# A fused attention and expert kernel: three of eighteen score steps kept whole instead of six, with work moved between ScalarE, VectorE and GpSimd

## Chip, core and metric

The kernel runs on one core of a Trainium2 chip. The metric is device time in microseconds (us) of one launch. Three runs of the kernel before took 906.69 us (median; 906.01 to 906.83).

## The reference

There are two stages. The first is attention over 4 batches and 8 heads (32 in all), with 1152 keys, 64 numbers per head, and queries averaged in pairs, so that 576 are left:

```
q_pool = q.reshape(B, H, S // 2, 2, D).mean(axis=3)
scores = matmul(q_pool, k.T) / sqrt(D);  scores -= max(scores, axis=-1)
attn = exp(scores);  attn /= sum(attn, axis=-1) + 1e-9
x = matmul(attn, v)
```

The second takes the 2304 rows of x (512 wide) through `h = x @ w_in`, `g = s * max(h, 0)**2 + b`, `out = g @ w_out`, with 2048 columns in between. Everything is float32.

## The kernel before

**Splitting.** A float32r matmul stands as one record in the trace, a plain float32 one as two (384 records for the 192 of L774). To keep accuracy with float32r the kernel splits a tile into a rounded part (names that end in h: `ph`, `kh`, `qh`, `xh`; for values `vv`) and what the rounding left (`pl`, `vl`), and multiplies high by high, high by low and low by high. The rounded part is a copy into a float32r tile (`hi_of`); the rest is a subtraction.

**Steps.** The attention goes head by head, each head in 9 steps of 128 keys (`NJ`), so that two heads, a pair, are 18 steps, numbered 0 to 17 here, and there are 16 pairs. `score_step` multiplies keys by queries (four float32r matmuls, L742) into a PSUM tile `s`, of which there are two: the scores of a step need the tile of the step two before. ScalarE takes the exponential from it. The table `KIND` says by step what follows:

- `w`, whole: one exponential into `pe` (L746), kept in float32. `value_step` multiplies it with the unsplit values `vf` by two float32 matmuls (L774).
- `v`: a rounded exponential `ph` (L751) and a full one in place in PSUM (L754); VectorE subtracts to `pl` (L757) and by that frees the tile `s`. `value_step` has six float32r matmuls (L780, L782, L784).
- `g`: the same, but the full exponential goes to `pe` in SBUF, which frees `s` at once, and GpSimd subtracts. The matmuls are the same six.

`value_step` runs three steps behind (`LAG`). TensorE also runs the units that find the row maximum ahead of time (`max_unit`, L687, one or two in a step); VectorE reduces them (L688).

**Preparation.** While a pair runs, the operands of the pair after the next are made, at steps that the table `PREP` gives: transposes on VectorE (`ka`, `kb`, `qt`), rounding (`ha`, `hb`, `qh`), the low parts on GpSimd (`kl`, `ql`), `qz0` and `qz1` (`q_blocks`: a rounded copy of 64 partitions by 512 queries that gathers every fourth, for the maximum units), `qm` (a corner copy on ScalarE), and the transfers into place `l0`, `l1` from the queue of SyncE. `FIRST` shifts some in the first pair. `prep_v` rounds the values of the next head (`vv`) and subtracts (`vl`), at steps 8 and 17 (`VS`). `XT` and `STA` say how many steps after their start the pieces of the normalisation and of a weight's conversion come.

Each engine runs its instructions strictly in the order written; the tables set that order. `later(k, fn)` writes fn's instructions k steps on.

Of the kernel before, what the change touches and what calls it, by code (L numbers as in the profile page):

```python
# [32 lines left out]
KB = 384  # L33


KIND = "wvwvgvwvg" + "vwgvwvwgv"

PP = (("ka", 2), ("kb", 3), ("ha", 3), ("hb", 4), ("qs", 3), ("qt", 4), ("qm", 5), ("qz", 5), ("qh", 6), ("ql", 7), ("kl", 7), ("l0", 8))
FIRST = {"qs": 4, "qt": 1, "qm": 1, "qh": 1, "qz": 1, "ql": 1, "l1": 4}
PREP = (("qs", 9), ("ka", 10), ("kb", 11), ("ha", 11), ("hb", 12), ("kl", 12), ("qt", 13), ("qm", 14), ("qh", 14), ("qz", 14), ("ql", 15), ("l0", 4), ("l1", 13))  # L40
LR = 14
LD = 5
VS = (8, 17)
XT = (2, 2, 3, 4, 8)
SW = (3, 8)
CB, CP = 270, 18
WB = (7, 7)
STA = (0, 1, 3, 5, 8, 9, 18, 19, 20)
STB = (0, 1, 2, 3, 4, 5, 5, 7, 9)
MO = (2, 3, 6)  # L50
MP = (1, 2, 3, 4, 6)
# [5 lines left out]
def f32(ap):  # L57
    return ap.bitcast(F32)
# [3 lines left out]
def attention_moe_kernel(ctx: ExitStack, tc: tile.TileContext, q, k, v, w_in, w_out, s_in, b_in, out):  # L62
    nc = tc.nc
# [5 lines left out]
    P = 128  # L69
# [3 lines left out]
    NT4 = SQ // P  # L73
# [217 lines left out]
    def hi_of(eng, out, in_):  # L291
        if eng is nc.scalar:
            nc.scalar.activation(out, in_, AF.Copy)  # L293
        else:
            eng.tensor_scalar(out=out, in0=in_, scalar1=1.0, scalar2=0.0, op0=ALU.mult, op1=ALU.add)
# [6 lines left out]
    def later(k, fn):  # L302
        step[1] += 1
        queue.append((step[0] + k, step[1], fn))
# [217 lines left out]
    qm = ap.tile([P, P], F32R, name="qm")  # L522

    qzs = [ap.tile([P, 2, NT4 * P], F32R, name=f"qz{i}") for i in range(2)]
# [4 lines left out]
    def side(hd, of="v"):  # L529

        h = hd % 2 if of == "v" else 1 - hd % 2
        return slice(h * D, (h + 1) * D)
# [19 lines left out]
    def load_q(p, which=(0, 1)):  # L552
        if p not in qraw:
            qraw[p] = ap.tile([P, NBQ, 2, 32], F32, tag="qraw", name=f"qraw{p}")
        for r, b, h, c in quarters(p):
            for e in which:
                eng = nc.sync if p > 1 or e == 0 else nc.scalar
                eng.dma_start(qraw[p][r, :, e], q[b, h, e::2, c].rearrange("(j t) i -> t j i", t=32))
# [6 lines left out]
    def prep_pair(p):  # L565

        kr, qr = kraw.pop(p), qraw.pop(p)
        kT = ap.tile([P, S], F32, tag="kT", bufs=2, name=f"kT{p}")
        qT = ap.tile([P, SQ], F32, tag="qT", bufs=2, name=f"qT{p}")
        qs = ap.tile([P, NBQ, 32], F32, tag="qs", name=f"qs{p}")  # L570
        kh = ap.tile([P, S], F32R, tag="kh", bufs=2, name=f"kh{p}")
        qh = ap.tile([P, SQ], F32R, tag="qh", bufs=2, name=f"qh{p}")
        krv = kr.rearrange("p j i -> p (j i)")
        lo, hi = (slice(0, SQ), slice(SQ, S)) if p else (slice(0, KB), slice(KB, S))

        def corner():
            assert holds.get("qm", -1) == p - 1
            for h in range(2):
                d = slice(h * D, (h + 1) * D)
                hi_of(nc.scalar, qm[d, d], qT[d, NT4 * P:])  # L580
            holds["qm"] = p

        def k_hi(part, last):
            hi_of(nc.scalar if p < 3 else nc.gpsimd, kh[:, part], kT[:, part])
            khs[p] = kh

        def q_hi():
            hi_of(nc.scalar if p < 2 else nc.gpsimd, qh, qT)
            qhs[p] = qh

        def q_blocks(h):
            r = slice(h * D, (h + 1) * D)
            to, of = qzs[p % 2][r, h], (f32(qh) if p == 0 and h else qT)[r, :NT4 * P]
            if p or h:
                hi_of(nc.scalar if p == 0 else nc.gpsimd, to.rearrange("p (t m) -> p t m", t=NT4), of.rearrange("p (m t) -> p t m", t=NT4))
            else:
                hi_of(nc.gpsimd, to, of)

        def both():
            q_blocks(0)  # L600
            q_blocks(1)

        def k_lo(part=slice(0, S)):
            nc.gpsimd.tensor_tensor(out=kT[:, part], in0=kT[:, part], in1=f32(kh[:, part]), op=ALU.subtract)

        def lay(h):
            hd = 2 * p + h
            kk, qq = kks[hd % 3], qqs[hd % 3].rearrange("p i a n -> p i (a n)")
            r = slice(h * D, (h + 1) * D)
            def k_hi_to(part):  # L610
                nc.sync.dma_start(f32(kk[0:D, :, part]), f32(kh[r, part]).unsqueeze(1).to_broadcast([D, 2, part.stop - part.start]))

            def k_lo_to(part):
                nc.sync.dma_start(f32(kk[D:P, 0, part]), kT[r, part])

            def q_hi_to():
                nc.sync.dma_start(f32(qq[0:D, 0, :]), f32(qh[r]))
                nc.sync.dma_start(f32(qq[D:P, 0, :]), f32(qh[r]))

            if hd == 0:  # L620
                for part in (lo, hi):
                    nc.sync.dma_start(f32(kk[0:D, 0, part]), f32(kh[r, part]))
                nc.scalar.activation(kk[0:D, 1], f32(kh[r]), AF.Copy)
                q_hi_to()
                k_lo_to(lo)
                k_lo_to(hi)
                nc.sync.dma_start(f32(qq[0:D, 1, :]), qT[r])
            else:
                k_lo_to(slice(0, S))
                k_hi_to(slice(0, S))  # L630
                q_hi_to()
                nc.sync.dma_start(f32(qq[0:D, 1, :]), qT[r])
            holds["k", hd % 3] = hd

        return {
            "ka": lambda: nc.vector.transpose(out=kT[:, lo], in_=krv[:, lo]),
            "qs": lambda: (nc.vector if p < 2 else nc.gpsimd).tensor_tensor(out=qs, in0=qr[:, :, 0, :], in1=qr[:, :, 1, :], op=ALU.add),
            "kb": lambda: nc.vector.transpose(out=kT[:, hi], in_=krv[:, hi]),  # L638
            "ha": lambda: k_hi(lo, False),
            "qt": lambda: nc.vector.transpose(out=qT, in_=qs.rearrange("p j i -> p (j i)")),  # L640
            "hb": lambda: k_hi(hi, True),
            "qh": q_hi,
            "qz": both,
            "qz0": lambda: q_blocks(0),
            "qz1": lambda: q_blocks(1),
            "kla": lambda: k_lo(lo),
            "klb": lambda: k_lo(hi),
            "kl": k_lo,
            "ql": lambda: nc.gpsimd.tensor_tensor(out=qT, in0=qT, in1=f32(qh), op=ALU.subtract),
            "qm": corner,  # L650
            "l0": lambda: lay(0),
            "l1": lambda: lay(1),
        }

    def prep_v(hd):
        vf, vv, vl = vfs[hd % 2][:, :, side(hd)], vvs[hd % 2][:, :, side(hd)], vls[hd % 2]
        if hd % 2:
            vl = vl[:, :, side(hd)]
        hi_of(nc.gpsimd, vv, vf)

        def lo():
            nc.gpsimd.tensor_tensor(out=vl, in0=vf, in1=f32(vv), op=ALU.subtract)  # L662
            holds["v", hd % 2] = hd

        later(1, lo)
# [123 lines left out]
    def finish(hd, a):  # L789
# [34 lines left out]
        if h == 0:  # L824
            later(XT[0], invert)
        else:
            for at, fn in zip(XT, (invert, reciprocal, spread, scale, send)):
                later(at, fn)
# [38 lines left out]
    for n in range(AHEAD):  # L867
        for u in range(begun(n - AHEAD), begun(n - AHEAD + 1)):
            max_unit(u, *((ps_m, "m") if u % 2 == 0 else (ps_s, "s")))
            if u == 1:  # L870
                prep["qz1"]()
                load_q(1, (1,))
                load_k(1)
                load_q(1, (0,))
                prep["l1"]()
                zeros(1)
                constants(1)
                prep_v(0)
                ones(1)
                constants(2)  # L880
        tick()
        if n == 11:
            prep = prep_pair(1)

    moe = Moe()
    lays = {}
    weights_a = conversions(wa, wstage, 0, SW[0], 1, STA, parts=2)
    NS = NH * NJ

    for n in range(NS + LAG):  # L890
# [5 lines left out]
        for part in ORDS.get(n % 18, ORD[at]) if at is not None else "sff":  # L896
            if part == "s" and n < NS:
                score_step(hd, j, KIND[n % 18])
            elif part == "f":
# [10 lines left out]
        if n < NS:  # L910
            p, h = divmod(hd, 2)
# [3 lines left out]
            if n == LD:  # L915
# [3 lines left out]
                load_q(2)  # L919
            if n % 18 == PREP[0][1]:  # L920
                lays = {k: prep[k] for k in ("l0", "l1") if k in prep}
                prep = prep_pair(p + 2) if p + 2 < NPAIR else {}
            for name, at in PREP:

                ops = prep if name not in ("l0", "l1") or at < PREP[0][1] else lays
                if n % 18 == at + (0 if p else FIRST.get(name, 0)) and name in ops and n >= 8:
                    ops.pop(name)()
# [134 lines left out]
```

## Time and profile before

| | us |
|---|---|
| median of 3 runs | 906.69 |
| the profiled execution | 906.96 |
| span of its core, first to last instruction | 905.1 |
| TensorE busy | 886.2 |
| VectorE busy | 690.8 |
| GpSimd busy | 637.2 |
| ScalarE busy | 573.9 |

The profiled execution spent 1.9 us outside its span. PE is the matmul side of TensorE and PEld its weight loads, DVE is VectorE, ACT ScalarE, POOL GpSimd, SP SyncE. The attention runs from about 20 to 500 us, the experts from there to the end. The granted clock of TensorE has mean 0.999 over the span.

### The profile page before, as it was taken

The numbers are of one execution on the slowest core, as the hardware profiler recorded it, in microseconds if no ns is written. First come the engines' busy times: TensorE is split into PE (matmuls) and PEld (weight loads), VectorE is DVE, ScalarE is ACT, GpSimd is POOL, SyncE is SP. The second block draws the span as 40 slices with busy tenths as digits, with TensorE's granted clock in tenths as the row PEclk, the third lists the DMA queues.
The fourth block names the chain that finished last, engine by engine and source line by source line (L and its number), as shares of the span: only waits on it lengthen the run. The fifth ranks groups of instructions, "written<-read, shape, count | busy, mean of one in ns | idle before, by whom it ended". The sixth has DMA issues, their size and how long they took to land.

```text
span 905.1 us, 17064 instructions
## 1 busy us (share of the span) xinstructions
PE 886.2 (98%) x6036; PEld 832.5 (92%) x6036; DVE 690.8 (76%) x1272; ACT 573.9 (63%) x1055; POOL 637.2 (70%) x541
## 2 busy tenths in 40 slices
PE   5999999999999999999999999999999999999997
PEld 3899999999999999999998899989999999999997
DVE  5888888889888988898874788789884456666666
ACT  3767667777776767776778677766664445454443
POOL 7767867887888788878856667579985445555443
PEclk9999999999999999999999999999999999999999
DMA  8889788877978797879563466766534222222111
GB/s 158 155 173 190 163 163 172 166 173 158 188 150 178 158 192 144 180 159 181 130 146 97 154 195 209 216 197 212 187 135 133 78 70 72 71 71 70 48 47 47
DMA packets 255733, 130.93 MB, mean 145 GB/s; under 512 B 203744, under 2 KB 227424, under 8 KB 255648
## 3 DMA queue, kind: packets, MB, share of 16 engines
q1 hardware_dynamic: 248544, 128.96, 60.2%
q10 hardware_dynamic: 7104, 0.89, 0.7%
q8 instruction: 48, 0.79, 0.4%
q14 instruction: 37, 0.30, 0.1%
HBM read 68.68 MB, written 18.87 MB: 97 GB/s over the span
## 4 chain that ended last, share of the span: by engine, by line
PE 94%; DVE 2%; ACT 1%; DMA 1%; POOL 1%; issue 0%; ACTq 0%; POOLq 0%; DVEq 0%
PE s L742 17%; PE h L412 11%; PE y L387 11%; PE h L360 11%; PE o L774 10%; PE seven L460 10%; PE m L687 8%; PE o L782 5%; PE o L784 5%; PE o L780 5%; DVE pm L688 1%; DMA kraw<-in_k_dram 0%; DMA qraw<-in_q_dram 0%; DVE kT L638 0%; DVE lt L802 0%
## 5 line engine op out<-in xcount | busy, mean ns | idle before, releaser
L688 DVE TENSOR_REDUCE pm<-m 128x1 f32<-128x384 f32 x432 | 227.6, 545 | 55.2 <-PE m L687 49.5
L742 PE MATMUL s<-qq,kk 128*128 128x288 f32 x1152 | 215.5, 309 | 1.9 <-DVE qq L716 1.3
L742 PEld LDWEIGHTS s<-qq,kk 128*128 128x128 f32 x1152 | 176.1, 190 | 13.9 <-ACT qq L714 1.6
L751 ACT ACTIVATE ph<-s 128x576 fp32r<-128x576 f32 x192 | 125.3, 653 | 91.9 <-PE s L742 91.1
L687 PE MATMUL m<-kh,qz 128*128 128x384 f32 x384 | 152.3, 409 | 0.5 <-DVE pm L688 0.5
L757 POOL TENSOR_TENSOR pl<-pe,ph 128x576 fp32r<-128x576 f32 x64 | 91.2, 1425 | 79.6 <-ACT pe L754 54.1
L774 PE MATMUL o<-pe,vf 128*128 128x288 f32 x384 | 120.9, 405 | 0.0
L757 DVE TENSOR_TENSOR pl<-s,ph 128x576 fp32r<-128x576 f32 x128 | 95.9, 749 | 23.0 <-ACT s L754 17.8
L782 PE MATMUL o<-ph,vl 128*64 128x288 f32 (+1 forms) x384 | 113.3, 295 | 0.2 <-POOL vl L662 0.2
L784 PE MATMUL o<-pl,vv 128*128 128x288 f32 x384 | 113.2, 295 | 0.1
L780 PE MATMUL o<-ph,vv 128*128 128x288 f32 x384 | 113.0, 294 | 0.0
L360 PE MATMUL h<-x,wih 128*128 128x256 f32 x576 | 106.8, 283 | 0.8 <-DVE gl L374 0.7
L412 PE MATMUL h<-x,wih 128*128 128x256 f32 x576 | 104.2, 281 | 0.0
L360 PEld LDWEIGHTS h<-x,wih 128*128 128x128 f32 x576 | 93.7, 190 | 7.7 <-DVE gl L374 1.9
L440 POOL TENSOR_TENSOR cl<-c,ch 128x640 fp32r<-128x640 f32 x35 | 54.9, 1567 | 56.3 <-ACT ch L436 56.3
L412 PEld LDWEIGHTS h<-x,wih 128*128 128x128 f32 x576 | 88.7, 188 | 0.2
L754 ACT ACTIVATE s<-s 128x576 f32<-128x576 f32 x128 | 83.6, 653 | 0.0
L687 PEld LDWEIGHTS m<-kh,qz 128*128 128x128 f32 x384 | 73.4, 194 | 9.3 <-DVE pm L688 2.9
L338 POOL TENSOR_TENSOR x<-xr,x 128x1024 fp32r<-128x1024 f32 x27 | 64.9, 2405 | 23.8 <-ACT x L293 23.8
L360 PE MATMUL h<-x,wil 128*128 128x256 f32 x288 | 81.6, 283 | 0.0
L412 PE MATMUL h<-x,wil 128*128 128x256 f32 x288 | 81.1, 282 | 0.0
L746 ACT ACTIVATE pe<-s 128x576 f32<-128x576 f32 x96 | 62.7, 653 | 25.7 <-PE s L742 21.2
(295 smaller groups left out, 2196.1 us busy)
## 6 DMA issues: line engine op xcount, KB each, us to landing
kk<-kh SPq DMA_DIRECT2D x31, 576.0 KB, 6.4
vf<-in_v_dram SPq DMA_DIRECT2D x32, 288.0 KB, 4.5
qq<-qh SPq DMA_DIRECT2D x64, 144.0 KB, 5.6
xr<-xd SPq DMA_DIRECT2D x18, 512.0 KB, 3.9
kk<-kT SPq DMA_DIRECT2D x31, 288.0 KB, 3.4
qraw<-in_q_dram SPq DMA_DIRECT2D x120, 72.0 KB, 2.5
kraw<-in_k_dram SPq DMA_DIRECT2D x60, 144.0 KB, 3.4
wsti<-in_moe_w_in_dram SPq DMA_DIRECT2D x13, 512.0 KB, 4.0
```

The source lines that it names most:

```text
L360: nc.tensor.matmul(h[:, :TB], st[:, c, :], mv[:, c, :], start=(n == 0), stop=(n == 3 * NC - 1))
L387: nc.tensor.matmul(y[:, :DM], st[:, ts_], mv, start=(first and n == 0), stop=(last and n == 2))
L412: nc.tensor.matmul(h[:, e * TB:(e + 1) * TB], st[:, c, :], mv[:, c, :], start=(k == 0), stop=(k == 3 * NC - 1))
L687: nc.tensor.matmul(ps[:, :KB], st, khs[p][:, e * KB:(e + 1) * KB], start=True, stop=True)
L688: nc.vector.tensor_reduce(out=pms[p][:, col, e:e + 1], in_=ps[:, :KB], axis=AX.X, op=ALU.max)
L742: nc.tensor.matmul(ps[:, a, :HALF], kk[:, i, j * P:(j + 1) * P], qq[:, i, a], start=(i == 0), stop=(i == 1))
L751: nc.scalar.activation(ph, ps[:, :, :HALF], AF.Exp, scale=SCALE)
L757: fresh.append(lambda: eng.tensor_tensor(out=pl, in0=full, in1=f32(ph), op=ALU.subtract))
L774: nc.tensor.matmul(o[:, :HALF], vfs[hd % 2][:, j], ph[:, a], start=first, stop=last)
L780: nc.tensor.matmul(o[:, :HALF], vv[:, j], ph[:, a], start=first, stop=False)
L782: nc.tensor.matmul(o[0:vl.shape[2], :HALF], vl[:, j], ph[:, a], start=False, stop=False)
L784: nc.tensor.matmul(o[:, :HALF], vv[:, j], pl[:, a], start=False, stop=last)
```

## The change

Four things are edited. `KIND` turns three whole steps of each pair into split ones: per pair 6 `w`, 8 `v`, 4 `g` become 3 `w`, 7 `v`, 8 `g`, with four `g` in a row at steps 1 to 4. The copies `qz0` and `qz1` go from GpSimd to ScalarE for every pair from the third on, and read `qh` instead of `qT`. The values' rounding `vv` goes from GpSimd to ScalarE. And `PREP`, `XT` and `STA` move pieces by a step. The diff in full:

```diff
--- before.py
+++ after.py
@@ -33,19 +33,19 @@
 KB = 384
 
 
-KIND = "wvwvgvwvg" + "vwgvwvwgv"
+KIND = "vggggwvvg" + "vgwwvgvgv"
 
 PP = (("ka", 2), ("kb", 3), ("ha", 3), ("hb", 4), ("qs", 3), ("qt", 4), ("qm", 5), ("qz", 5), ("qh", 6), ("ql", 7), ("kl", 7), ("l0", 8))
-FIRST = {"qs": 4, "qt": 1, "qm": 1, "qh": 1, "qz": 1, "ql": 1, "l1": 4}
-PREP = (("qs", 9), ("ka", 10), ("kb", 11), ("ha", 11), ("hb", 12), ("kl", 12), ("qt", 13), ("qm", 14), ("qh", 14), ("qz", 14), ("ql", 15), ("l0", 4), ("l1", 13))
+FIRST = {"qs": 4, "qt": 1, "qm": 1, "qh": 1, "qz0": 1, "ql": 1, "l1": 4}
+PREP = (("qs", 9), ("ka", 9), ("kb", 10), ("ha", 10), ("hb", 11), ("kl", 12), ("qt", 13), ("qh", 13), ("qm", 14), ("ql", 14), ("qz0", 15), ("qz1", 15), ("l0", 4), ("l1", 12))
 LR = 14
 LD = 5
 VS = (8, 17)
-XT = (2, 2, 3, 4, 8)
+XT = (1, 2, 3, 5, 8)
 SW = (3, 8)
 CB, CP = 270, 18
 WB = (7, 7)
-STA = (0, 1, 3, 5, 8, 9, 18, 19, 20)
+STA = (0, 1, 4, 5, 8, 10, 18, 19, 20)
 STB = (0, 1, 2, 3, 4, 5, 5, 7, 9)
 MO = (2, 3, 6)
 MP = (1, 2, 3, 4, 6)
@@ -590,9 +590,9 @@
 
         def q_blocks(h):
             r = slice(h * D, (h + 1) * D)
-            to, of = qzs[p % 2][r, h], (f32(qh) if p == 0 and h else qT)[r, :NT4 * P]
+            to, of = qzs[p % 2][r, h], (f32(qh) if p > 1 or (p == 0 and h) else qT)[r, :NT4 * P]
             if p or h:
-                hi_of(nc.scalar if p == 0 else nc.gpsimd, to.rearrange("p (t m) -> p t m", t=NT4), of.rearrange("p (m t) -> p t m", t=NT4))
+                hi_of(nc.gpsimd if p == 1 else nc.scalar, to.rearrange("p (t m) -> p t m", t=NT4), of.rearrange("p (m t) -> p t m", t=NT4))
             else:
                 hi_of(nc.gpsimd, to, of)
 
@@ -656,7 +656,7 @@
         vf, vv, vl = vfs[hd % 2][:, :, side(hd)], vvs[hd % 2][:, :, side(hd)], vls[hd % 2]
         if hd % 2:
             vl = vl[:, :, side(hd)]
-        hi_of(nc.gpsimd, vv, vf)
+        hi_of(nc.scalar, vv, vf)
 
         def lo():
             nc.gpsimd.tensor_tensor(out=vl, in0=vf, in1=f32(vv), op=ALU.subtract)
```

ScalarE's instructions around the end of a pair (steps 14 to 17, and step 0 of the next), before; in a name such as `pe19_6` the first number is the head and the second its step of nine, so that `19_6` is step 15 of the pair and `20_0` step 0 of the next:

```order
L751 ACTIVATE ph19_5_4382<-s19_5_4377 128x576
L754 ACTIVATE s19_5_4377<-s19_5_4377 128x2x288
L293 ACTIVATE qm_100<-qT11_4275 64x64 x2
L746 ACTIVATE pe19_6_4423<-s19_6_4418 128x576
L751 ACTIVATE ph19_7_4441<-s19_7_4435 128x576
L754 ACTIVATE pe19_7_4440<-s19_7_4435 128x576
L751 ACTIVATE ph19_8_4459<-s19_8_4454 128x576
L754 ACTIVATE s19_8_4454<-s19_8_4454 128x2x288
L746 ACTIVATE pe20_0_4481<-s20_0_4476 128x576
L219 ACTIVATE whmo1a_4493<-wsto1a_4066 128x256
```

After the change, the same place on ScalarE:

```order
L293 ACTIVATE qm_100<-qT11_4515 64x64 x2
L751 ACTIVATE ph19_6_4665<-s19_6_4660 128x576
L754 ACTIVATE s19_6_4660<-s19_6_4660 128x2x288
L293 ACTIVATE qz1_102<-qh11_4518 64x512 x2
L751 ACTIVATE ph19_7_4683<-s19_7_4677 128x576
L754 ACTIVATE pe19_7_4682<-s19_7_4677 128x576
L751 ACTIVATE ph19_8_4705<-s19_8_4700 128x576
L754 ACTIVATE s19_8_4700<-s19_8_4700 128x2x288
L293 ACTIVATE vv0_105<-vf0_103 128x9x64
L751 ACTIVATE ph20_0_4727<-s20_0_4722 128x576
L754 ACTIVATE s20_0_4722<-s20_0_4722 128x2x288
L219 ACTIVATE whmo1a_4746<-wsto1a_4294 128x256
```

Step 15 was whole, with one exponential, and is now split with two; behind it stand two `qz1` copies, ahead of the exponentials of step 16; a `vv` copy stands ahead of those of step 0.

GpSimd's instructions from the end of step 17 to step 8, before (`w...` tiles are those of a weight's conversion):

```order
L295 TENSOR_SCALAR vv0_105<-vf0_103 128x9x64
L250 TENSOR_TENSOR wRi1a_3646<-wRi1a_3646,wabi1a_3644 128x256
L662 TENSOR_TENSOR vl0_107<-vf0_103,vv0_105 128x576
L253 TENSOR_TENSOR wAi1a_3645<-wAi1a_3645,wih0_269 128x256
L256 TENSOR_TENSOR wil0_271<-wAi1a_3645,wRi1a_3646 128x2x128
L757 TENSOR_TENSOR pl18_4_4151<-pe18_4_4149,ph18_4_4150 128x576
L819 TENSOR_TENSOR xo8_4190<-xu16_3879,rr8_4173 64x576
L819 TENSOR_TENSOR xo8_4190<-xu17_4098,rr8_4173 64x576
L757 TENSOR_TENSOR pl18_8_4239<-pe18_8_4237,ph18_8_4238 128x576
L295 TENSOR_SCALAR vv1_106<-vf1_104 128x9x64
L662 TENSOR_TENSOR vl1_108<-vf1_104,vv1_106 128x9x64
```

After the change, the same place on GpSimd:

```order
L250 TENSOR_TENSOR wRi1a_3849<-wRi1a_3849,wabi1a_3847 128x256
L662 TENSOR_TENSOR vl0_107<-vf0_103,vv0_105 128x576
L253 TENSOR_TENSOR wAi1a_3848<-wAi1a_3848,wih0_269 128x256
L757 TENSOR_TENSOR pl18_1_4310<-pe18_1_4308,ph18_1_4309 128x576
L256 TENSOR_TENSOR wil0_271<-wAi1a_3848,wRi1a_3849 128x2x128
L757 TENSOR_TENSOR pl18_2_4340<-pe18_2_4338,ph18_2_4339 128x576
L757 TENSOR_TENSOR pl18_3_4362<-pe18_3_4360,ph18_3_4361 128x576
L757 TENSOR_TENSOR pl18_4_4389<-pe18_4_4387,ph18_4_4388 128x576
L819 TENSOR_TENSOR xo8_4448<-xu16_4102,rr8_4411 64x576
L819 TENSOR_TENSOR xo8_4448<-xu17_4327,rr8_4411 64x576
L757 TENSOR_TENSOR pl18_8_4481<-pe18_8_4479,ph18_8_4480 128x576
L662 TENSOR_TENSOR vl1_108<-vf1_104,vv1_106 128x9x64
```

Two `vv` copies have left, four subtractions `pl18_1` to `pl18_4` stand where one did, and the scaling `xo8` follows behind them.

## Rows read from the trace of the kernel before

**Rows 1.** The page's section 4: the chain of waits by engine.

```profile
PE 94%; DVE 2%; ACT 1%; DMA 1%; POOL 1%; issue 0%; ACTq 0%; POOLq 0%; DVEq 0%
```

**Rows 2.** By stretch, one pair: us, PE, PEld, DVE, ACT, POOL busy, PEclk, DMA, GB/s.

```profile
171.45:201.31 29.86, 29.86 (x198) 28.16 (x197) 25.93 (x49) 21.40 (x40) 24.74 (x22) 1.00 0.84 170
```

**Rows 3.** The scores' group by line: busy us, mean ns | idle us before, releasers.

```profile
L742 PE MATMUL s<-qq,kk 128*128 128x288 f32 x1152 | 215.5, 309 | 1.9 <-DVE qq L716 1.3 <-ACT pe L746 0.3 <-DVE pl L757 0.2
```

**Rows 4.** TensorE's timeline: start us, us, instruction.

```profile
195.29 0.34 PE L687 MATMUL m<-kh,qz 128*128 128x384 f32 x1
195.47 0.30 PE L782 MATMUL o<-ph,vl 128*128 128x288 f32 x1
...
202.49 0.65 PE L774 MATMUL o<-pe,vf 128*128 128x288 f32 x2
...
204.25 0.29 PE L780 MATMUL o<-ph,vv 128*128 128x288 f32 x1
...
205.04 0.29 PE L780 MATMUL o<-ph,vv 128*128 128x288 f32 x1
...
210.22 1.13 PE L774 MATMUL o<-pe,vf 128*128 128x288 f32 x4
```

**Rows 5.** Timeline of all engines: how work is handed over in a step.

```profile
183.01 0.80 PE L742 MATMUL s<-qq,kk 128*128 128x288 f32 x4
...
192.96 0.70 PE L742 MATMUL s<-qq,kk 128*128 128x288 f32 x4
...
193.70 0.66 ACT L746 ACTIVATE pe<-s 128x576 f32<-128x576 f32 x1
...
197.40 0.74 DVE L757 TENSOR_TENSOR pl<-s,ph 128x576 fp32r<-128x576 f32 x1
...
197.86 0.80 PE L742 MATMUL s<-qq,kk 128*128 128x288 f32 x4
...
209.27 0.65 ACT L754 ACTIVATE pe<-s 128x576 f32<-128x576 f32 x1
...
210.00 1.41 POOL L757 TENSOR_TENSOR pl<-pe,ph 128x576 fp32r<-128x576 f32 x1 [1.51 <-DMA qraw<-in_q_dram]
...
210.48 0.65 ACT L751 ACTIVATE ph<-s 128x576 fp32r<-128x576 f32 x1 [0.56 <-PE s L742]
...
211.02 0.65 ACT L754 ACTIVATE s<-s 128x576 f32<-128x576 f32 x1
```

**Rows 6.** Groups by line and shape: what one moved instruction takes.

```profile
L757 DVE TENSOR_TENSOR pl<-s,ph 128x576 fp32r<-128x576 f32 x128 | 95.9, 749 | 23.0 <-ACT s L754 17.8 <-PE s L742 3.5
L757 POOL TENSOR_TENSOR pl<-pe,ph 128x576 fp32r<-128x576 f32 x64 | 91.2, 1425 | 79.6 <-ACT pe L754 54.1 <-issue 20.1 <-DMA qraw<-in_q_dram 3.0
L295 POOL TENSOR_SCALAR qz<-qT 64x512 fp32r<-64x512 f32 x31 | 34.0, 1097 | 3.8 <-DVE qT L640 2.6
L295 POOL TENSOR_SCALAR vv<-vf 128x576 fp32r<-128x576 f32 x32 | 21.6, 675 | 1.0 <-DMA vf<-in_v_dram 0.9
L293 ACT ACTIVATE kh<-kT 128x576 fp32r<-128x576 f32 x4 | 2.7, 686 | 0.2 <-DVE kT L638 0.2
L623 ACT ACTIVATE kk<-kh 64x1152 fp32r<-64x1152 f32 x1 | 1.1, 1147 | 0.0
L293 ACT ACTIVATE qz<-qh 64x512 fp32r<-64x512 f32 x1 | 1.1, 1129 | 0.0
```

**Rows 7.** SyncE's own timeline, steps 10 to 17 of a pair.

```profile
188.45 0.94 SPq L563 DMA_DIRECT2D vf<-in_v_dram  x1
193.88 0.51 SPq L727 DMA_DIRECT2D qq<-c  x1
...
195.08 0.59 SPq L614 DMA_DIRECT2D kk<-kT  x1
...
199.88 0.83 SPq L632 DMA_DIRECT2D qq<-qT  x1
```

**Rows 8.** DMA issues by line: count, KB each, median us to landing.

```profile
vf<-in_v_dram SPq DMA_DIRECT2D x32, 288.0 KB, 4.5
```

## The prediction

> **What bounds the kernel now.** I read the chain of waits first: 94% of it is TensorE [rows 1]. Then one pair in the middle of the attention, by stretch: 29.86 us, of which the matmul side is busy all 29.86, VectorE 25.93, GpSimd 24.74 and ScalarE 21.40, at a granted clock of 1.00 [rows 2]. A busy matmul side can hide gaps, so I looked at the groups and the timeline: in the whole run the score matmuls were held up for 1.9 us [rows 3], and in the pair two score groups took 0.80 us where 0.70 is usual [rows 5], about 0.1 us lost each. So in the attention time follows TensorE's work, and what an engine beside it does is free as long as the scores and the split products are not made late. The experts are untouched.
>
> **TensorE's own work.** Six float32r matmuls of a split step run from 204.25 to 205.04, 0.79 us. Of a whole step two records in a row take 0.65 us and four 1.13; ends are modelled, but the two more cost 0.48, so 0.24 each and 0.96 for the step's four [rows 4]. A step turned from whole to split saves 0.17 us. Three steps by 16 pairs are 48: **-8.2 us**. A pair would take 29.86 - 0.51 = 29.35 us.
>
> **VectorE** loses one `pl` of 0.75 us a pair [rows 6]; being off the path that is worth nothing by itself. **GpSimd** gains four `pl` of 1.425 and loses two `qz` of 1.097 and two `vv` of 0.675 [rows 6]: +5.70 - 2.19 - 1.35 = +2.16, 26.9 of 29.35 us. It still fits, and what counts is each result's due time. A `g` step's `pl` is due three steps on. In the four steps in a row GpSimd needs 1.4 us for each, a step of TensorE lasts about 1.6, and a weight's piece of about 1 us and `xo` stand between or behind. From its scores' start a `pl` is ready for GpSimd after 0.74 us (192.96 to 193.70) and two exponentials (0.54 to the next, 0.65, and 0.08 for the hand-over, 209.27 + 0.65 to 210.00) [rows 5], 2.0 in all, and done at 3.4 if the engine is free; it is wanted after three steps and 1 us, 5.8. There are 2.4 us of cover, of which a backlog of one instruction takes 1.4. I take 0; if the cover is gone, see the rivals.
>
> **ScalarE** gains three exponentials, two `vv` and two `qz`. A `vv` was never run there; the nearest row is the copy of as many columns, `kh` at 0.686 us. A `qz` ran there once, 1.129 us [rows 6]. Back to back the next starts 0.11 before the end (210.48 + 0.65 to 211.02) [rows 5], so 3 by 0.54, 2 by 0.58 and 2 by 1.02 make +4.8: 26 of 29.35 us. On average there is room. But ScalarE works strictly in order and the two `qz` stand together between the exponentials of step 15 and those of step 16. This is the place on which the forecast rests.
>
> I work it out with t = 0 at the start of step 15's scores. A maximum unit takes 0.18 us (195.29 to 195.47) [rows 4] and four scores 0.53. Step 15 carries the product of step 12 (whole) and one unit, 0.53 + 0.96 + 0.18 = 1.67; step 16 a split and two units, 1.68; step 17 a split and one, 1.50. So scores start at 0, 1.67, 3.35 and 4.85 (step 0). ScalarE: step 15's exponentials start at 0.74 and 1.28, the `qz` at 1.82 and 2.84, step 16's at 3.86 and 4.40, ending at 5.05. Without `qz` they would have started at 2.41. Step 0's scores need the tile `s` of step 16 at 4.85 and get it at about 5.12: **0.27 us lost**. Step 17's exponentials follow at 4.94 and 5.48, ending at 6.13. Step 17 is a `v` step, so VectorE's `pl`, 6.21 to 6.96, frees its tile. Step 1's scores, due at 5.12 + 1.68 = 6.80, start at about 7.03: **0.23 us lost**. The `vv` at 6.02 moves step 0's exponentials to 6.60. Between the scores of steps 1 and 2 stand the products of two steps, and the backlog ends there. That is 0.50 us a pair. It comes in the 14 pairs in which a pair from the third on is prepared: **+7.0 us**.
>
> The old loss at step 16 (197.86, behind the `pl` that ends at 198.14 [rows 5]) goes, since step 14 is now a `g`: 0.1 by 14, **-1.4 us**. I leave the other at 183.01 as it is.
>
> Bounds of what the trace does not show: if a `qz` on ScalarE took what its columns cost elsewhere (`kk`, 1152 columns in 1.147, `kh`, 576 in 0.686 [rows 6]: 0.8 ns a column, so 512 take 0.63), step 16 would end at 4.05 and nothing be lost, 0 us. If `qz` takes longer in the middle of the attention than at the start, both losses grow by as much; 1.0 us a pair, +14, is the other end. I take the row of the same shape, 1.129. The `vv` copy lies between 0.5 (its columns alone) and 1.1 (as if gathered); at 0.69 it takes 0.58 of the queue, and a split step leaves ScalarE 1.5 to 1.68 less two by 0.54, 0.4 to 0.6 us. So alone, as at step 8, it costs 0; after step 17 it is in the sum above.
>
> [...]
>
> **The rest of the order.** `l1`, five transfers, goes one step earlier and so ahead of the `vf` load on SyncE. It issues in 5.6 us (195.08 to 199.88 + 0.83), mostly into time in which SyncE waited for `c` until 193.88 [rows 7]. `vf` moves from 188.45 to about 194.1, lands 4.5 us later [rows 8], and `vv` needs it after step 17's exponentials, about 202: 3 us of cover, 0 us. Transfers behind it come earlier. The pieces moved by `XT` and `STA` keep their engines: 0 us. In the last pair no units run, the steps are shorter and GpSimd has four more `pl`; there I allow up to 0.5 us either way and take 0.
>
> **Sum.** -8.2 + 7.0 - 1.4 = -2.6 us. The profiled execution took 906.96 us (905.1 of span and 1.9 around it), so 904.4; the median of the runs is 0.27 lower: **904.1 us**. With losses of 0.3 to 0.7 us a pair the forecast's own range is 901.5 to 907.
>
> **Rivals.**
>
> A. ScalarE absorbs it: a `qz` there is cheaper, or the tiles come free sooner than I have it. Then -8.2, with -1.4 to -2.8 of the two old losses: 895.7 to 897.1, say 897. For it: ScalarE has 3 us free in a pair, and my sum has 0.27 and 0.23 only, each the difference of long queues. Against it: the row of 1.129.
>
> B. Slower: ScalarE's backlog from `qz` and `vv` doesn't end at step 2. Price: with 1.0 us a pair, -8.2 + 14 - 1.4 = +4.4, 911. It turns slower from 0.7 us lost a pair (8.2 + 1.4 over 14). For it: everything that frees a score tile passes ScalarE, and three of five instructions before it in the queue are new. Against it: the long stretch between the scores of steps 1 and 2, and four `g` steps, which free `s` without VectorE.
>
> C. GpSimd is late in the row of `g` steps. From `wR` to `pl` of step 4 are nine instructions, about 11 us against some 12 that TensorE gives them; 2.4 us of cover, so it decides if they run about a fifth longer or start late. At 0.35 us a pair more, 14 pairs: +4.9, 909. Against it: durations on GpSimd hardly move (1.41 and 1.425 [rows 5, 6]).
>
> **How the numbers follow.** Forecast 0.50, A 0.22, B 0.18, C 0.10. What a measurement can tell from no change is 0.2%, 1.8 us: 904.9 to 908.5. Of the forecast's 0.50, 0.28 lies below that and 0.22 within. A is all faster; of B 0.14 slower and 0.04 within; of C 0.05 each. Faster 0.50, within 0.31, slower 0.19. The range 896.5 to 910 leaves out the lower half of A and the upper half of B, about 0.2.
>
> **What would show it.** Right: matmuls of L774 halved, from 384 to 192 records; `qz` on ScalarE near 1.13 us; a pair near 29.7 us; the score groups of steps 0 and 1 held up behind `pe` and `pl`. Wrong: a pair near 29.2 with no wait of scores (A), near 30.3 with waits in more steps (B), or split products L784 waiting for GpSimd's `pl` (C).

## The result, and the profile after

The changed kernel takes **911.81 us** (median of 4 runs, 910.58 to 912.33), the kernel before 906.76 beside it (906.01 to 906.99). The ratio is 1.0055, with a 95% interval of 1.0038 to 1.0073: slower by about 5 us, where 904.1 us and a gain of 2.6 had been forecast.

The page's chain of waits, by engine, to be held against [rows 1]. TensorE has lost four points of it; VectorE, ScalarE, GpSimd and the DMA queues have each gained one:

```profile
PE 90%; DVE 3%; ACT 2%; POOL 2%; DMA 2%; issue 1%; ACTq 0%; POOLq 0%; SPq 0%; DVEq 0%
```

By stretch, the changed kernel: the second pair and the sixth (us, then busy time of PE, PEld, DVE, ACT and POOL, the granted clock, DMA share, GB/s). The sixth is the pair that [rows 2] show of before.

```profile
50.81:84.38 33.57, 30.61 (x205) 28.51 (x203) 24.48 (x45) 25.52 (x45) 23.77 (x18) 1.00 0.92 188
174.89:205.06 30.17, 29.65 (x201) 28.19 (x201) 25.18 (x47) 26.05 (x47) 26.70 (x21) 1.00 0.80 167
```

The granted clock is the same (1.00 in both stretches), so it isn't that. The sixth pair takes 30.17 us instead of 29.86, and TensorE is idle in 0.52 us of it, where before it was busy throughout. The second pair is a case of its own: 33.57 us, 30.06 before.

Groups of the page (busy us, mean ns | idle us before, and what ended it), to be held against [rows 3] and [rows 6]:

```profile
L742 PE MATMUL s<-qq,kk 128*128 128x288 f32 x1152 | 207.6, 302 | 10.4 <-ACT pe L754 6.4 <-DVE qq L716 1.3 <-DVE pl L757 1.3
L757 POOL TENSOR_TENSOR pl<-pe,ph 128x576 fp32r<-128x576 f32 x128 | 187.2, 1473 | 63.8 <-ACT pe L754 27.7 <-issue 23.6 <-DMA qraw<-in_q_dram 7.6
L757 DVE TENSOR_TENSOR pl<-s,ph 128x576 fp32r<-128x576 f32 x112 | 84.7, 756 | 51.5 <-ACT s L754 49.8 <-issue 0.4
L784 PE MATMUL o<-pl,vv 128*128 128x288 f32 x480 | 141.9, 296 | 0.9 <-POOL pl L757 0.7
L774 PE MATMUL o<-pe,vf 128*128 128x288 f32 x192 | 61.7, 405 | 0.0
L293 ACT ACTIVATE qz<-qh 64x512 fp32r<-64x512 f32 x29 | 33.0, 1137 | 0.5
L293 ACT ACTIVATE vv<-vf 128x576 fp32r<-128x576 f32 x32 | 21.9, 686 | 4.5 <-DMA vf<-in_v_dram 2.5 <-DMA qraw<-in_q_dram 1.7
```

The change did what it says: L774 has half its records, GpSimd twice as many `pl`, and `qz` and `vv` are on ScalarE near the durations that the forecast took (1.129 and 0.686). But the score matmuls now wait 10.4 us where they had waited 1.9, and 6.4 of it is for ScalarE's second exponential, `pe` of L754.

The place, in the timeline of the changed kernel (start, us, instruction [idle before, releaser]), from step 15's scores at 199.57 to step 1's at 207.03:

```profile
199.57 0.69 PE L742 MATMUL s<-qq,kk 128*128 128x288 f32 x4
...
200.30 0.65 ACT L751 ACTIVATE ph<-s 128x576 fp32r<-128x576 f32 x1
...
200.84 0.65 ACT L754 ACTIVATE s<-s 128x576 f32<-128x576 f32 x1
...
201.02 0.91 PE L742 MATMUL s<-qq,kk 128*128 128x288 f32 x4
201.51 2.29 ACT L293 ACTIVATE qz<-qh 64x512 fp32r<-64x512 f32 x2
...
202.91 0.69 PE L742 MATMUL s<-qq,kk 128*128 128x288 f32 x4
203.82 0.65 ACT L751 ACTIVATE ph<-s 128x576 fp32r<-128x576 f32 x1
...
204.36 0.65 ACT L754 ACTIVATE pe<-s 128x576 f32<-128x576 f32 x1
...
205.06 0.80 PE L742 MATMUL s<-qq,kk 128*128 128x288 f32 x4 [0.49 <-ACT pe L754]
...
206.13 0.76 DVE L757 TENSOR_TENSOR pl<-s,ph 128x576 fp32r<-128x576 f32 x1 [1.62 <-ACT s L754]
...
207.03 0.77 PE L742 MATMUL s<-qq,kk 128*128 128x288 f32 x4
```

This is the stretch that the prediction counted from t = 0 at step 15's scores. Step 16's `ph` starts at t = 4.25, where 3.86 was worked out, and step 0's scores at 5.49, where they were due at 4.85.

The second pair, in the same view: SyncE issues a `vf` load, ScalarE's `vv` waits for it, and two steps' exponentials, VectorE's `pl` and the next scores wait behind that. Those two steps' scores had started at 66.83 and 68.33 and took 0.69 and 0.70 us; the first exponential starts at 70.05.

```profile
65.41 0.52 SPq L563 DMA_DIRECT2D vf<-in_v_dram  x1
...
69.46 0.68 ACT L293 ACTIVATE vv<-vf 128x576 fp32r<-128x576 f32 x1 [2.49 <-DMA vf<-in_v_dram]
70.05 0.63 ACT L751 ACTIVATE ph<-s 128x576 fp32r<-128x576 f32 x1
...
71.33 0.76 DVE L757 TENSOR_TENSOR pl<-s,ph 128x576 fp32r<-128x576 f32 x1 [2.90 <-ACT s L754]
...
72.23 0.76 PE L742 MATMUL s<-qq,kk 128*128 128x288 f32 x4 [1.27 <-DVE pl L757]
```

Pair lengths, from the first score matmul of a pair to that of the next (pairs counted from 0), and the time that TensorE's starts stand apart beyond the work between them, as a mean over pairs 4 to 12:

| kernel | pair 0 | 1 | 2 | later, typical | lost a pair | at which scores |
|---|---|---|---|---|---|---|
| before | 34.28 | 30.06 | 29.88 | 29.85 | 0.26 | steps 7, 16: 0.10 each |
| after | 33.57 | 33.57 | 30.20 | 30.17 | 1.12 | steps 0: 0.75, 1: 0.27, 3: 0.09 |

From this the budget can be read. A steady pair loses 0.86 us more and its work is 0.54 shorter: +0.32, in pairs 2 to 13 together +3.7. Pair 1 costs +3.5. The start of the first scores, pair 0 and the last two pairs give back 1.5. Together +5.7 at the start of the last scores, and the profiled spans differ by 5.4 (910.5 and 905.1).

### The profile page after: what moved, and what is told of

The parts are those of the page before. It is cut to its first block, busy times and chain, and to the rows that moved or that the text cites. A ratio compares the mean times of both kernels' runs of the same rounds, so it can differ in the third digit from the quotient of the medians.

```text
span 910.5 us, 17663 instructions
## 1 busy us (share of the span) xinstructions
PE 882.6 (97%) x6132; PEld 833.8 (92%) x6132; DVE 680.9 (75%) x1256; ACT 643.6 (71%) x1163; POOL 674.4 (74%) x545
## 4 chain that ended last, share of the span: by engine, by line
PE 90%; DVE 3%; ACT 2%; POOL 2%; DMA 2%; issue 1%; ACTq 0%; POOLq 0%; SPq 0%; DVEq 0%
PE s L742 17%; PE h L412 11%; PE y L387 11%; PE h L360 11%; PE seven L460 10%; PE m L687 8%; PE o L780 6%; PE o L784 6%; PE o L782 6%; PE o L774 5%; ACT ph L751 1%; DVE pm L688 1%; ACT pe L754 1%; POOL pl L757 1%; DMA vf<-in_v_dram 0%
## 5 line engine op out<-in xcount | busy, mean ns | idle before, releaser
L757 POOL TENSOR_TENSOR pl<-pe,ph 128x576 fp32r<-128x576 f32 x128 | 187.2, 1473 | 63.8 <-ACT pe L754 27.7
L742 PE MATMUL s<-qq,kk 128*128 128x288 f32 x1152 | 207.6, 302 | 10.4 <-ACT pe L754 6.4
L751 ACT ACTIVATE ph<-s 128x576 fp32r<-128x576 f32 x240 | 156.0, 650 | 56.5 <-PE s L742 49.6
L784 PE MATMUL o<-pl,vv 128*128 128x288 f32 x480 | 141.9, 296 | 0.9 <-POOL pl L757 0.7
L782 PE MATMUL o<-ph,vl 128*64 128x288 f32 (+1 forms) x480 | 141.5, 295 | 0.0
L780 PE MATMUL o<-ph,vv 128*128 128x288 f32 x480 | 140.8, 293 | 0.0
L757 DVE TENSOR_TENSOR pl<-s,ph 128x576 fp32r<-128x576 f32 x112 | 84.7, 756 | 51.5 <-ACT s L754 49.8
L784 PEld LDWEIGHTS o<-pl,vv 128*128 128x128 f32 x480 | 90.1, 188 | 5.7 <-POOL pl L757 1.6
L780 PEld LDWEIGHTS o<-ph,vv 128*128 128x128 f32 x480 | 90.1, 188 | 0.0
L754 ACT ACTIVATE pe<-s 128x576 f32<-128x576 f32 x128 | 83.2, 650 | 0.0
```

Of the source, the lines that this page charges most:

```text
L742: nc.tensor.matmul(ps[:, a, :HALF], kk[:, i, j * P:(j + 1) * P], qq[:, i, a], start=(i == 0), stop=(i == 1))
L751: nc.scalar.activation(ph, ps[:, :, :HALF], AF.Exp, scale=SCALE)
L754: nc.scalar.activation(full, ps[:, :, :HALF], AF.Exp, scale=SCALE)
L757: fresh.append(lambda: eng.tensor_tensor(out=pl, in0=full, in1=f32(ph), op=ALU.subtract))
L780: nc.tensor.matmul(o[:, :HALF], vv[:, j], ph[:, a], start=first, stop=False)
L782: nc.tensor.matmul(o[0:vl.shape[2], :HALF], vl[:, j], ph[:, a], start=False, stop=False)
```

## The experiments

All are edits of the changed kernel. The kernel before was timed on the same chip each time: 906.88, 906.77 and 907.07 us in the three groups of runs.

**1. The query copies back on GpSimd** (its copies of the second pair were there already):

```diff
-hi_of(nc.gpsimd if p == 1 else nc.scalar, to.rearrange(...
+hi_of(nc.scalar if p == 0 else nc.gpsimd, to.rearrange(...
```

> The changed kernel with the two qz copies back on GpSimd (they still read qh). Theory Q (the two qz copies in a row hold up ScalarE's queue, and with it the score tiles of steps 16 and 17): the waits of the score matmuls of steps 0, 1 and 3, 1.1 us a pair in the changed kernel, go; a steady pair takes 29.2 to 29.5 us instead of 30.17, the whole 897 to 900 us. Theory G (GpSimd is too full since it has eight subtractions a pair): GpSimd gets 2.2 us more a pair, so it stays at 911 us or gets slower, with split products waiting for pl.

904.15 us (903.87 to 905.48), ratio to before 0.9965 [0.9953, 0.9977]: 7.7 less than the changed kernel. The loss at steps 0 and 1 is gone. But the pairs fall into two kinds. By stretch, one pair without and one with weight pieces of the experts on GpSimd:

```profile
140.66:169.91 29.25, 29.25 (x204) 28.09 (x202) 25.48 (x48) 24.00 (x45) 26.98 (x21) 1.00 0.82 172
...
199.64:229.39 29.75, 29.63 (x204) 28.16 (x202) 25.08 (x48) 23.99 (x45) 29.04 (x24) 1.00 0.81 168
```

In the second, GpSimd is busy 29.04 of 29.75 us. It has become the bound there, and split products wait for its `pl` (0.24 us a pair at step 5 alone).

**2. The query copies on ScalarE, but apart**, at steps 1 and 5:

```diff
-PREP = (... ("ql", 14), ("qz0", 15), ("qz1", 15), ("l0", 4), ("l1", 12))
+PREP = (... ("ql", 14), ("l0", 4), ("l1", 12), ("qz0", 1), ("qz1", 5))
```

(`qz0` leaves `FIRST` as well, here and in runs 7, 9 and 10.)

> The changed kernel with both qz copies still on ScalarE, but apart and later: qz0 at step 1 and qz1 at step 5 (a whole step with one exponential) of the next pair, not both at step 15. Theory Q in its form 'it is the two together, ahead of a v step, that cost': a pair of 29.2 to 29.6 us, the whole 898 to 902. If instead ScalarE simply has too much work in a pair, the wait moves to other steps and the time stays at 908 to 912.

903.91 us (903.2 to 904.08), ratio 0.9961 [0.9946, 0.9976]: between the two expectations. Pairs of 29.58; the loss moved to the scores of steps 4 (0.29) and 8 (0.17), and halved.

**3. The values' rounding back on GpSimd:**

```diff
-        hi_of(nc.scalar, vv, vf)
+        hi_of(nc.gpsimd, vv, vf)
```

> The changed kernel with the values' rounding vv back on GpSimd, qz as changed. Theory V (vv on ScalarE stands in its queue waiting for the transfer of vf, 2.5 us once in the second pair, and adds to the backlog at step 1): the second pair falls from 33.6 to about 30.5 us and a steady pair from 30.17 to about 29.9 (the 0.27 at step 1 goes, the 0.75 at step 0 stays): 911.8 - 3 - 3.5 = 904 to 906. If vv is harmless: 911 to 912, and GpSimd's 1.3 us more may show as waits for pl.

911.32 us (910.85 to 911.77), ratio 1.0044 [1.0029, 1.0059]. The later pairs stay at 30.17 with the same losses at steps 0 and 1 (0.76 and 0.27). So `vv` has no part in a steady pair's loss. Pair 1 fell from 33.57 to 31.49, but pair 0 (34.52) and pair 2 (30.76) grew by 1.5 together: the fall of the total that was expected from pair 1 alone didn't come.

**4. Both back on GpSimd** (edits 1 and 3 together):

> The changed kernel with both qz and vv back on GpSimd: the new division of steps and the new order alone. Theories Q and V together: every saving of TensorE is kept, a pair of 29.3 us and the second pair near 30, 895 to 898. Theory G: GpSimd has 24.7 + 5.7 = 30.4 us of work in a pair of 29.3 and becomes the bound: a pair of 30.5 us or more in the middle, 912 to 920.

919.99 us (919.69 to 920.46), ratio 1.0140 [1.0123, 1.0157], with pairs of 31.04. Products of `pl` and `vv` wait 0.69 us at step 1 and 0.61 at step 5. GpSimd is late with eight `pl`, `qz` and `vv`: in the whole run L784 waited 12.3 us for `pl`, against 0.7 in the changed kernel. With `qz` on GpSimd, moving `vv` to ScalarE is worth 15.8 us (run 4 less run 1).

**5. The same copies, read straight.** From the third pair on the copy reads its 512 columns in a row instead of every fourth; what is left out is the reordering of the queries that the maximum units see, everything else keeps its place.

```diff
-..., of.rearrange("p (m t) -> p t m", t=NT4))
+..., (of.rearrange("p (m t) -> p t m", t=NT4) if p < 2 else of.rearrange("p (t m) -> p t m", t=NT4)))
```

> The changed kernel, but from the third pair on qz0 and qz1 read qh straight on instead of every fourth float (left out: the reordering of queries for the maximum units, so the maxima belong to other queries). Theory S (a gathered read costs ScalarE twice): two copies take about 1.2 us instead of 2.29, the waits at steps 0 and 1 fall from 1.0 us to 0.1 to 0.2, a pair of 29.3 to 29.5 us, the whole 898 to 902. If the copies cost what they cost for another reason (64 partitions, float32r output): unchanged, 911 to 912.

897.53 us (897.21 to 898.68), ratio 0.9899 [0.9884, 0.9913]. In the timeline of this kernel, the place from step 15's exponentials to step 0's scores:

```profile
195.16 0.65 ACT L754 ACTIVATE s<-s 128x576 f32<-128x576 f32 x1
...
195.83 1.28 ACT L293 ACTIVATE qz<-qh 64x512 fp32r<-64x512 f32 x2
...
197.12 0.65 ACT L751 ACTIVATE ph<-s 128x576 fp32r<-128x576 f32 x1
...
197.67 0.65 ACT L754 ACTIVATE pe<-s 128x576 f32<-128x576 f32 x1
...
198.73 0.69 PE L742 MATMUL s<-qq,kk 128*128 128x288 f32 x4
```

Two copies take 1.28 us instead of 2.29, step 16's exponentials end at 198.32, and step 0's scores come without a wait. Pairs are 29.16, with 0.11 lost. This is the run that decides: 1.01 us less of copies, 1.01 less lost in a pair, 14 pairs, -14.3 us.

**6. The old mix of steps**, everything else as after:

```diff
-KIND = "vggggwvvg" + "vgwwvgvgv"
+KIND = "wvwvgvwvg" + "vwgvwvwgv"
```

> The changed kernel with the old division of steps (6 whole, 8 by VectorE, 4 by GpSimd); qz and vv stay on ScalarE, the order stays. Theory Q: step 15 is then whole, with one exponential, so ScalarE has 0.54 us more time around qz, and step 16's pair of exponentials still waits; TensorE has 0.51 us more work a pair. The waits should be smaller than the changed kernel's 1.1 us, 0.3 to 0.7, and a pair 29.9 to 30.2 us: 907 to 911. It says what moving qz and vv costs by itself.

918.42 us (917.89 to 919.39), ratio 1.0130 [1.0113, 1.0147]: above what was expected. Pairs of 30.58 lose 0.98, at five scores (steps 0, 1, 5, 7, 16), where 0.3 to 0.7 had been expected: with step 15 whole the loss is not much below the changed kernel's 1.12. So the moved copies and roundings, together with the pieces moved by a step (which no run put back by themselves), cost 11.7 us against the kernel before; the new mix gives 6.6 of them back.

**7. The query copies on ScalarE at steps 3 and 4:**

```diff
+PREP = (... ("ql", 14), ("l0", 4), ("l1", 12), ("qz0", 3), ("qz1", 4))
```

> The changed kernel with qz0 at step 3 and qz1 at step 4 of the next pair, on ScalarE. There, g steps free their score tile by ScalarE's second exponential and step 5 is whole, so 1.16 us of backlog should be gone before step 6, a v step. With qz at steps 1 and 5 a pair lost 0.29 at step 4 and 0.17 at step 8; if the place in the order is what counts, both go: a pair of 29.1 to 29.3 us, the whole 897 to 900. If ScalarE's total work counts, 903 to 905 as with steps 1 and 5.

**901.31 us** (901.04 to 902.1), ratio 0.9939 [0.9925, 0.9954]: the fastest version that computes the whole reference, 5.5 us below the kernel before and 10.5 below the changed one. The time lies between the two expectations: place counts, but not all of the loss went. Pairs are 29.40, with 0.34 lost, 0.27 of it at step 8. ScalarE and the scores in the timeline of this kernel, from step 4's scores (177.25) to step 8's (183.78):

```profile
177.25 0.69 PE L742 MATMUL s<-qq,kk 128*128 128x288 f32 x4
177.72 1.13 ACT L293 ACTIVATE qz<-qh 64x512 fp32r<-64x512 f32 x1
178.75 0.64 ACT L751 ACTIVATE ph<-s 128x576 fp32r<-128x576 f32 x1
...
179.28 0.64 ACT L754 ACTIVATE pe<-s 128x576 f32<-128x576 f32 x1
179.94 1.14 ACT L293 ACTIVATE qz<-qh 64x512 fp32r<-64x512 f32 x1
...
180.41 0.69 PE L742 MATMUL s<-qq,kk 128*128 128x288 f32 x4
181.11 0.65 ACT L746 ACTIVATE pe<-s 128x576 f32<-128x576 f32 x1
...
182.88 0.76 DVE L757 TENSOR_TENSOR pl<-s,ph 128x576 fp32r<-128x576 f32 x1 [0.62 <-ACT s L754]
...
183.78 0.77 PE L742 MATMUL s<-qq,kk 128*128 128x288 f32 x4
```

The second copy stands before step 5, a whole step with one exponential (L746) and not two. Nothing is late until step 8, which wants the tile that VectorE's `pl` frees at 183.64.

**8. One rounding on GpSimd**, that of head 3, which waited for the `vf` load in pair 1:

```diff
-        hi_of(nc.scalar, vv, vf)
+        hi_of(nc.gpsimd if hd == 3 else nc.scalar, vv, vf)
```

> The changed kernel with one of its 32 roundings of values, head 3's (prepared in the second pair, where ScalarE waited 2.49 us for the transfer of vf), back on GpSimd. Theory: that wait stands in ScalarE's queue ahead of the exponentials of steps 9 and 10 of the second pair, which is why this pair's steps 10 to 13 take 2.3 us longer there than in the later pairs; on GpSimd the wait is beside the scores. So the second pair goes from 33.57 to about 31.3 to 32 us, the later pairs stay at 30.17, and the total falls by 1.2 to 2.3 us, to 909.5 to 910.6. Rival: GpSimd is late then, as in the kernel with all of vv on it, where the second pair gained but the first and third lost 1.5 together: the later pairs stay at 30.17 and the total falls by 0.5 or less.

910.1 us (909.96 to 910.26, 5 runs), ratio 1.0032 [1.0019, 1.0045]. Pair 1 goes from 33.57 to 31.02, pair 2 grows by 0.2, the later ones stay. So this one wait cost about 1.7 us of the run by the two medians (2.0 if each is taken against the kernel before beside it). The same rounding in this kernel's timeline:

```profile
64.31 0.52 SPq L563 DMA_DIRECT2D vf<-in_v_dram  x1
...
68.40 0.67 POOL L295 TENSOR_SCALAR vv<-vf 128x576 fp32r<-128x576 f32 x1
```

It starts as long after its load's issue (4.1 us) as on ScalarE, but no exponential stands behind it.

**9. Runs 7 and 8 together:**

> The kernel with the query copies at steps 3 and 4 (901.3 us) with head 3's rounding of the values on GpSimd as well. There the wait of ScalarE for vf in the second pair is 1.79 us and steps 10 to 13 of that pair take 1.65 us longer than in later pairs. Theory: that goes, the later pairs stay at 29.40, total 899.4 to 900.3. Rival (GpSimd late): no change, 900.8 to 901.6.

901.44 us (900.19 to 902.2, 5 runs), ratio 0.9934 [0.9922, 0.9947]: no gain over run 7 that the runs can tell. Pair 1 fell by 1.70 us, from 31.34 to 29.64, but pair 2 rose by 1.06. The rival's number came, but not by its mechanism, late GpSimd. The first scores of pair 2 wait for a transfer instead, in this kernel's timeline:

```profile
79.06 0.59 SPq L728 DMA_DIRECT2D qq<-c  x1
...
81.52 0.67 PE L742 MATMUL s<-qq,kk 128*128 128x288 f32 x3 [0.79 <-DMA qq<-c]
```

In run 7 that transfer was issued at 79.35 and step 0's scores began at 82.44, without a wait. Here they began at 80.44, 2.0 us sooner, and the transfer was issued only 0.3 sooner: these scores lost 1.05 us, which is pair 2's growth. SyncE issues `qq<-c` behind the five transfers of `l1`, which the change had moved up a step; before, `qq<-c` went first in this pair (74.44, `l1` from 75.66). No run put `l1` back.

**10. The copies one step earlier than in run 7**, at steps 2 and 3 (`("qz0", 2), ("qz1", 3)`):

> The query copies on ScalarE one step earlier, at steps 2 and 3 instead of 3 and 4. At steps 3 and 4 all but 0.34 us of a pair's loss is gone; what is left is 0.27 us at step 8's scores, which wait for the exponentials of the steps whole on ScalarE's and VectorE's side (6 and 7). Theory: what is left is ScalarE's backlog not yet worked off at step 6; a step more to work it off in takes 0.1 to 0.27 us from each of 14 pairs, pair 29.15 to 29.3, total 897.5 to 900. Rival: the steps 3 to 6 are no place of slack any more than 2 is, the loss moves to step 4 (as 0.29 us did with copies at steps 1 and 5), pair 29.4 or more, total 901 to 904.

910.14 us (909.77 to 911.24, 5 runs), ratio 1.0034 [1.0021, 1.0048]: a clear miss, 8.8 us slower than run 7 by one step's shift. In the timeline of this kernel, from step 4's scores to step 6's:

```profile
179.20 0.69 PE L742 MATMUL s<-qq,kk 128*128 128x288 f32 x4
...
180.83 1.13 ACT L293 ACTIVATE qz<-qh 64x512 fp32r<-64x512 f32 x1
...
181.99 0.65 ACT L751 ACTIVATE ph<-s 128x576 fp32r<-128x576 f32 x1
182.54 0.64 ACT L754 ACTIVATE pe<-s 128x576 f32<-128x576 f32 x1
...
183.24 0.79 PE L742 MATMUL s<-qq,kk 128*128 128x288 f32 x4 [0.59 <-ACT pe L754]
```

Both copies now stand ahead of the two exponentials of step 4, the last of the four `g` steps, and step 6's scores wait for the second exponential: 0.87 us a pair. In run 7 only one copy stood ahead of them. "Earlier" was the wrong thing to look for; what counts is how much of the queue stands ahead of the exponential that frees a tile soon wanted.

## Why the prediction was wrong

The step that failed is the term for ScalarE's queue at steps 15 to 1: "0.50 us a pair ... **+7.0 us**". Its place was right and its size was not: 0.75 us at step 0's scores where 0.27 was worked out, 0.27 at step 1's where 0.23 was, 1.02 a pair and some 14.3 us in 14 pairs. The total is rival B's, 911, which had been priced at 1.0 us a pair, but B's mechanism did not come: waits were to spread to more steps, and they stayed at steps 0 and 1, behind `pe` and `pl`, as the forecast had said. The 0.09 at step 3 stands in run 5 too (0.11), without the long copies, and `vv`, which B counted in, adds nothing to a steady pair (run 3). That the sum meets 911 so closely is in part luck: pair 1's +3.5 was in no one's sum, and 1.5 at the start and the end and a second old loss stood against it.

Where the 0.48 at step 0 comes from can be read off the timeline after:

- The prediction let each instruction on ScalarE start 0.11 before the end of the last, as two exponentials do [rows 5], and so put the two `qz` 1.02 apart. Here the first starts 0.02 after the exponential ahead of it (200.84 + 0.65 to 201.51), the two take 2.29, and `ph` follows at 203.82. Three overlaps that don't occur, about 0.12 us each, and 0.02 of longer copies make step 16 later by 0.39 (4.25 less 3.86).
- Step 0's score group, which waited, took 0.80 us (205.06) instead of 0.69; the prediction had read this 0.1 as a loss in [rows 5], but did not add it to its own two waits.

0.27 + 0.39 + 0.11 is 0.77, against 0.75 measured. That the copies do it is shown by run 5, not only argued: with them 1.01 us shorter and nothing moved, the loss goes from 1.12 to 0.11. In that run the loss fell as much as the queue ahead of it, 1.01 us each; so an error of about 0.12 at each of three places came out whole, 14 times over.

The other terms:

- **TensorE's -8.2.** Right. From run 5 the work of a pair without its losses is 29.16 - 0.11 = 29.05, before 29.85 - 0.26 = 29.59: 0.54 a pair, where 0.51 was worked out. Over 16 pairs that is -8.6.
- **The old losses, -1.4.** Both went, not one: 0.20 a pair; a new 0.09 at step 3 took part of it.
- **`vv` on ScalarE, 0.** Right for a steady pair (run 3). The "3 us of cover" was worked out from the middle of the attention alone. In pair 1 there was none: 2.49 us of wait, worth 1.7 us (run 8). In the kernel before the same wait stood in GpSimd's queue, 0.9 us of it [rows 6], and in that pair no score waited for it.
- **GpSimd, 0, and rival C.** Right for the version as changed: its products (L784) waited 0.7 us for `pl` in the whole run. Runs 1 and 4 show how near the bound is: with `qz` back on GpSimd it sets the time of the pairs with weight pieces (29.75 us, against 29.25 of a pair without).
- **The row of the gathered copy.** The row of 1.129 held (1.137, 29 times), and run 5 shows the same columns in a row at 0.632. The price of gathering is 0.50 us for these 512 columns; why a gathered read takes longer was not shown.
- **The rest of the order, 0.** Right for a steady pair of the changed kernel, where no score waits for a transfer. In pair 2 a transfer that now stands behind `l1` cost 1.05 us once the scores came sooner (run 9), and the wait for it stands there in runs 3 (0.6) and 8 (0.2) too.
- **Rival A, 897.** Run 5 gives that time, 897.53: it is what the change would have made if the copy cost what its columns do. The prediction's bound at "0 us" for this case was sound.

What stays open: why the copies of run 7 overlapped their neighbours in part (the first, 177.72 to 178.75, is 1.03 apart; the second, 179.94 to 181.11, is 1.17). It is regular: in runs 2, 7, 9 and 10 the copy `qz0`, on partitions 0 to 63, overlaps the instructions on both sides of it by about 0.1 us in each of the 14 pairs, and `qz1`, on partitions 64 to 127, neither. No run tried what decides it.

## What to carry to other kernels

When work moves to an engine with room on average, find for each place in its queue the first result behind it that another engine wants soon, and sum the queue with the spacing of those very instructions, not that of their neighbours; where the slack was near zero, a change of the queue came out whole, once a repetition (1.01 us of copies, 1.01 us of loss in run 5). Put the long instruction ahead of the step with the least work behind it: here one step's shift was worth 8.8 us. Work out a load's cover in the first repetitions as well as in the steady one, and keep an instruction that may wait for a load off the queue that frees the bound engine's buffers; here one such wait was worth 1.7 us (run 8).

## What the runs showed of the hardware

- On ScalarE a copy of 64x512 float32 that reads every fourth element takes 1.137 us (mean of 29, the changed kernel), one that reads them in a row 0.632 (run 5).
- Two such copies in a row, gathered or not, were not overlapped, as two exponentials of 0.65 us were that started 0.54 apart (200.30 and 200.84): 2.29 us for two of 1.137, 1.28 for two of 0.632.
- Three `pl` in a row on GpSimd took longer than three single ones. The changed kernel's timeline, a single one and the three of steps 2 to 4:

```profile
174.91 1.43 POOL L757 TENSOR_TENSOR pl<-pe,ph 128x576 fp32r<-128x576 f32 x1 [1.88 <-ACT pe L754]
...
181.35 4.59 POOL L757 TENSOR_TENSOR pl<-pe,ph 128x576 fp32r<-128x576 f32 x3
```

That is 1.53 each on average: the first took 1.44 us, as a single one, the second 1.63 and the third 1.61. The group's mean is 1.473, where it was 1.425 [rows 6]. The cause was not tried.
